# Two classical groups of gate and up instead of three, twelve by seven products; VectorE or GpSimd chosen while the list is made

## The chip, the cores and the metric

The kernel runs on one core of a Trainium2 chip. Its engines are TensorE (PE, with its weight loads shown apart as PEld), VectorE (DVE), ScalarE (ACT) and GpSimd (POOL), and SyncE (SP), whose queue issues the DMAs. Each engine works through its own instructions in the order in which they are written and waits on semaphores. The metric is the device time of one execution in microseconds (us), the median of several runs.

## What is computed

One transformer block in float32: 2048 tokens of 448 features, attention over a sliding window of 256 keys with 16 heads of 28, then a gated feed-forward network with 1792 inner features.

```
h = x + attention(layernorm(x)) @ wo      # wqkv: 448 -> 3*448, causal, window 256
n = layernorm(h)
out = h + (gelu(n @ w_gate) * (n @ w_up)) @ w_down   # 448 -> 1792 -> 448
```

## The kernel before

Every float32 operand of a matmul is held as a high part and a low part (`to_hi` on ScalarE, `to_lo` on VectorE or GpSimd: the rest that the high part leaves), and a product is the sum of three matmuls: high by high, high by low, low by high.

**The list.** The kernel first describes all its work as operations (`op(engine, cost, latency, key, function, reads, writes, ...)`) with tokens for what each reads and writes. Then `Lists.run` makes the order: it keeps a clock for each engine, takes the operation that can begin first (among those that can begin nearly at once, the one with the smallest key) and writes its instructions. The order of every engine is thus a result of the costs and keys in the table of constants at the top. Where PE would stand idle early on, `idle` puts in a 128 x 128 transpose that computes nothing (line 1720). An operation marked `port` is kept from beginning while the other of VectorE and GpSimd holds the port between them, by the list's clock.

**The stages.** Layer norm of the 16 token tiles and transposition into `xT` (`layer_norms`, `normalise`); projections to q and k (line 678) and values (line 624); 16 blocks of scores, maxima, exponentials and sums (lines 729, 802, 840), whose parts are keyed against each other; output projection (line 900), which is added to `hres` on VectorE (line 903). `MERGE` says for each of the last twelve blocks whether its attend step runs in one piece or two.

**The feed-forward network** goes through 14 groups, each a pair of 128-feature slices of gate and up for 1024 tokens (2 x 512). A group is done in one of two ways:

- Classical (the first `CL` groups): four turns, each one of gate or up for 512 tokens. A turn is seven slots of six matmuls on half the rows (`cslot`, line 1139), or full-height ones in the first three turns (`cfull`, line 1151). The weights come as sets `cw_set` and the tokens through `tokens_c`.
- By seven products (all others): one level of a Strassen-like scheme over 2 x 2 blocks, so that two units (gate and up) share 25 slots of two products each, three pairs of matmuls in a slot (`both`, line 1340). It needs sums of tokens (`tokens_x(0)` for the first 1024 tokens, `tokens_x(1)` for the others) and sums of weights (`weight_set`: five sums `sum_` at line 1210 on GpSimd, then five splits), and it adds up partial products from the banks: `copied` on ScalarE (1346), `added` on VectorE (1350), `finished`.

Both ways end in the same step: gelu(gate) * up is split into `gh`, `e` or `xT` buffers and multiplied by the down weights (`down_half`, line 1414), in halves of 12 matmuls that are put between the slots (`pause`), and `out_add` (line 1431, VectorE) adds four banks to `hres` and stores them when they are final. `seen` (line 1260) is a one-element ScalarE read that tells the change of a bank from one half of the array to the other.

The buffers of the tokens for the first round of products lie in `late`, which opens only when all attention and output projections are through (token `fp`); a weight set may come into `proj` or `ev` only when the token `wosfree` says the same of the output projection:

```
opened = ["evenring", "wvfree", "pkfree", "wosfree"]
key0 = key
for k in parts:
    key = key0 + (0 if cp else XSTEP * k)
```

## Time and profile before

| | us |
|---|---|
| median of 3 runs (696.35 to 698.05) | 696.68 |
| the profiled execution | 698.2 |
| its span, first to last instruction | 696.5 |
| PE busy | 685.1 |
| VectorE busy | 513.4 |
| ScalarE busy | 413.9 |
| GpSimd busy | 311.1 |

The profiled execution lies 1.5 us above the median, and 1.7 us of it lie outside its span. The page's busy time is a mean over stages; it is to be read with the stretches of the kernel: the start (0 to 14 us), attention (to about 300), the mix of the last attention blocks with the classical groups (300 to 376), the seven-product groups (to 674) and the tail. In a timeline's row stand the start, the length, the engine, the line and operation, what is written from what, the count, and in brackets the idle time ahead and what ended it. In the chain of waits a row of PE without a row of another engine ahead of it waited for nothing but PE itself.

### The profile page before, as it was taken

Reading aid. Unit: us, or ns where it says so; the run is one execution under the profiler, and the core shown is the slowest. Engines: PE = TensorE matmul, PEld = TensorE weight load, DVE = VectorE, ACT = ScalarE, POOL = GpSimd, SP = SyncE. Lnnn points to the kernel's source line nnn. Section 1 sums busy time; section 2 is a strip of 40 time slices with the busy share of each in tenths; the row PEclk is TensorE's granted clock in tenths of the full one; section 3 lists DMA queues with packets and bytes.
Section 4 is the critical chain, followed back from the end, with each engine's and each line's share of the span. In section 5 each row is a group of like instructions: output and inputs, shape, how many; then the busy total and the mean of one; then the engine's idle time right before and its main releaser. Section 6 shows DMA issues by size and latency. Waiting matters only on the chain. (4 is left out here: it accounts for less than half of the span.)

```text
span 696.5 us, 15373 instructions
## 1 busy us (share of the span) xinstructions
PE 685.1 (98%) x5544; PEld 578.1 (83%) x5544; DVE 513.4 (74%) x1213; ACT 413.9 (59%) x911; POOL 311.1 (45%) x422
## 2 busy tenths in 40 slices
PE   8999999999999999999999999999999999999997
PEld 7888888888888878878878888888888888888886
DVE  7967678987798788838775789776555756866764
ACT  7747576877768667776554565644534545546431
POOL 5612654644456446441452779634303445447000
PEclk9999999999999999999999999999999999999999
DMA  9997967688688697406767775415004744533102
GB/s 315 277 285 216 286 173 202 183 230 244 166 210 247 183 273 207 165 1 178 197 181 158 213 205 170 119 51 171 20 16 131 211 132 132 161 116 88 44 15 105
DMA packets 104691, 116.25 MB, mean 167 GB/s; under 512 B 44632, under 2 KB 82392, under 8 KB 104040
## 3 DMA queue, kind: packets, MB, share of 16 engines
q1 hardware_dynamic: 104472, 115.17, 58.0%
q8 instruction: 43, 0.70, 0.4%
q14 instruction: 32, 0.26, 0.1%
q10 hardware_dynamic: 144, 0.11, 0.0%
HBM read 84.97 MB, written 44.47 MB: 186 GB/s over the span
## 5 line engine op out<-in xcount | busy, mean ns | idle before, releaser
L733 DVE CUSTOM_DVE_ANT_0 mt<-bank,mt 128x384 bf16<-128x384 f32 (+2 forms) x256 | 126.4, 526 | 26.8 <-PE bank L729 24.8
L806 ACT ACTIVATE pp<-bank 128x384 f32<-128x384 f32 (+1 forms) x188 | 90.8, 527 | 18.5 <-PE bank L802 16.3
L678 PE MATMUL bank<-xT 128*128 128x512 f32 x308 | 96.1, 399 | 0.0
L1340 PE MATMUL bank<-xT,proj 64*128 64x512 f32 x735 | 94.7, 389 | 0.2 <-DVE v L1350 0.2
L1340 PEld LDWEIGHTS bank<-xT,proj 64*128 64x128 f32 x735 | 72.1, 184 | 13.4 <-DVE v L1350 0.8
L729 PE MATMUL bank<-rk,rq 84*128 84x384 f32 (+2 forms) x256 | 81.0, 337 | 0.0
L802 PE MATMUL bank<-rq,rk 104*128 104x384 f32 (+2 forms) x352 | 80.6, 302 | 0.0
L821 POOL TENSOR_SCALAR_AFFINE_SELECT pp<-pp 128x512 f32<-128x512 f32 x96 | 60.6, 651 | 40.2 <-ACT pp L806 38.6
L1414 PE MATMUL bank<-proj,gh 64*128 64x448 f32 x624 | 71.5, 362 | 1.2 <-ACT e L1260 1.2
L802 PEld LDWEIGHTS bank<-rq,rk 104*128 104x128 f32 x352 | 59.4, 190 | 9.3 <-ACT pp L806 1.5
L1431 DVE TENSOR_TENSOR hres<-bank,hres 128x448 f32<-128x448 f32 (+1 forms) x113 | 62.8, 611 | 5.6 <-PE bank L1414 5.6
L1414 PEld LDWEIGHTS bank<-proj,gh 64*128 64x128 f32 x624 | 59.2, 184 | 8.0 <-ACT e L1260 1.9
L678 PEld LDWEIGHTS bank<-xT 128*128 128x128 f32 x308 | 55.6, 189 | 6.8 <-DVE proj L399 0.5
L1210 POOL TENSOR_TENSOR xn<-proj 64x128 f32<-64x128 f32 (+2 forms) x36 | 33.3, 928 | 52.5 <-DMA proj<-gu 46.8
L1260 ACT ACTIVATE e<-bank 1x1 f32<-1x1 f32 x139 | 21.7, 156 | 55.9 <-PE bank L1414 41.3
L729 PEld LDWEIGHTS bank<-rk,rq 84*128 84x128 f32 x256 | 47.6, 189 | 7.0 <-DVE mx L733 1.4
L396 ACT ACTIVATE rq<-bank 8x512 fp32r<-8x512 f32 x64 | 37.7, 589 | 22.1 <-PE bank L760 21.0
L399 DVE TENSOR_TENSOR proj<-proj 128x448 fp32r<-128x448 f32 (+2 forms) x42 | 25.8, 630 | 32.0 <-ACT proj L396 27.0
L624 PE MATMUL bank<-proj,xT 128*128 128x448 f32 (+1 forms) x220 | 49.1, 334 | 0.0
L1340 PE MATMUL bank<-xo,proj 64*128 64x512 f32 x366 | 47.7, 389 | 0.1
L1340 PEld LDWEIGHTS bank<-xo,proj 64*128 64x128 f32 x366 | 36.0, 184 | 7.1 <-DVE v L1350 0.8
L1350 DVE TENSOR_TENSOR raw<-bank,raw 128x512 f32<-128x512 f32 x22 | 15.2, 691 | 35.1 <-PE bank L1340 35.0
(193 smaller groups left out, 1474.3 us busy)
## 6 DMA issues: line engine op xcount, KB each, us to landing
rk<-k SPq DMA_DIRECT2D x44, 336.0 KB
rq<-q SPq DMA_DIRECT2D x32, 336.0 KB
gu<-in_gu_dram SPq DMA_DIRECT2D x18, 480.0 KB
proj<-gu SPq DMA_DIRECT2D x24, 288.0 KB
q<-proj SPq DMA_DIRECT2D x12, 448.0 KB
proj<-down SPq DMA_DIRECT2D x22, 224.0 KB
proj<-gu SPq DMA_DIRECT2D x24, 192.0 KB
k<-proj SPq DMA_DIRECT2D x9, 448.0 KB
```

The lines of the kernel that those rows point to most:

```text
L396: nc.scalar.activation(dst, src, AF.Copy)
L624: op("pe", mm(224 * n), 0.29 if n == 1 else 0.38, key + a / 16, lambda a=a, h=h, wb=wb, xb=xb: nc.tensor.matmul(bank[b.k][:, 0:224 * n], x ...
L678: op("pe", mm(512) + 0.002, 0.403, key, lambda a=a, h=h, wb=wb, xb=xb: nc.tensor.matmul(bank[b.k], wqk[m][:, h, wb, :], xT[:, xb, cc * 128 ...
L729: nc.tensor.matmul(bank[b.k][:, o:384], rq[u][0:3 * DH, j, i * 128:i * 128 + 128], rk[u][0:3 * DH, j, m0 * 128:(i + 3) * 128], start=True, ...
L733: nc.vector.tensor_tensor_reduce(junk[s % 2][:, o:384], bank[b.k][:, o:384], mask[:, o:384], 1.0, -BIG, OP.add, OP.max, mx[:, i, j:j + 1])
L802: nc.tensor.matmul(bank[b.k][:, n * i:n * i + n], rk[u][0:104, j + i, m * 128:m * 128 + 128], rq[u][0:104, j + i, lo * 128:(hi + 1) * 128] ...
L806: nc.scalar.activation(pp_cols(o, n)[:, j:j + G], bank[b.k][:, 0:G * n].rearrange("p (g t) -> p g t", g=G), AF.Exp, scale=SCALE)
L821: nc.gpsimd.affine_select(a, a, pattern=[[0, 4], [-cm, 128]], compare_op=op_, fill=0.0, base=0, channel_multiplier=cm)
L1210: arith("pool", w, key + 1, lambda e: e.tensor_tensor(xn_m[HALF[side], o:o + w], a(), b(), op=what), rd, [tok])
L1340: nc.tensor.matmul(bank[b.k], w, xarea(u.cp, xl, xs, side)[:, xk], start=p in (1, 2, 5) and not k and not t, stop=t == 2, tile_position=(6 ...
L1414: nc.tensor.matmul(bank[banks[q].k][:, 0:D], h[oh][0]()[HALF[x], q * 128:q * 128 + 128], d[wh][0]()[HALF[x]], start=not ph and not y and n ...
L1431: op("dve", 0.07 + w * 0.463 / D, 0.163 + w * 0.463 / D, key, lambda: nc.vector.tensor_tensor(hres[:, t, c0:c0 + w], bank[b.k][:, c0:c0 + ...
```

## The change

1. `CL` goes from 3 to 2: one group less is done classically and one more by seven products. The first product slot stands earlier in PE's order. The rings of buffers are arranged anew (`wbuf`, `cgbuf`, `SPARE`), and part of the token areas of the first round now lies in `xT` (`XPLACE`), where some of its loads may be made before attention ends (`X0LOAD`, `X0HOLD`).
2. An operation can have `alts`: engines with a cost each. The list then chooses the one on which it would end first; GpSimd counts only if no VectorE operation that holds the port began later than GpSimd could begin. `FLEX = 'xwc'` says for which: token sums and splits (x), weight sums and splits (w), copies from banks (c, ScalarE or VectorE).
3. Layer norm of the first tile (`QUICK = 1`): VectorE subtracts and scales in one instruction from the mean itself, so that one GpSimd step is left out.
4. The high and low halves of `xT` have tokens of their own (`XTB`), so that values and projections wait for the half that each matmul reads.
5. The list's cost for a DMA is changed, and nearly all keys in the table of constants are others.

```diff
-MERGE = (1, 1, 1, 0, 1, 1, 1, 1, 0, 1, 1, 1)
+MERGE = (1, 1, 1, 0, 1, 1, 1, 1, 1, 0, 0, 1)
...
-CL = 3
-CWL = 100
+FLEX = 'xwc'
+CL = 2
+CWL = -50
...
+QUICK = 1
+XFIRST = 4
...
+        if alts:
+            o.fn = lambda: alts[o.eng][2]()
...
+                if o.alts:
+                    ways = [x for x in o.alts if x != "pool" or began <= max(free[x], o.ready) + 0.02]
+                    if e not in ways or min(start_of(x, o)[0] + o.alts[x][1] for x in ways) < t + o.alts[e][1]:
+                        continue
...
-                bus = max(bus, t + 1.2) + o.size * 0.0034 + (1.25 if len(dmas) == 2 else 0)
+                bus = max(bus, t + 1.2) + o.size * (0.0028 if t < 15 else 0.0034) + (1.0 if len(dmas) == 2 else 0)
...
+                if e == "dve":
+                    began = t
...
+    def XTB(t, xb):
+
+        return span("xT", t, 1) if xb == 3 else span("xT", t + (xb > 3) / 2, 0.5)
...
+        if kind == "ln1" and t < QUICK:
+            op("dve", 0.45, 0.53, key, lambda: nc.vector.tensor_scalar(
+                xn[i2], hres[:, t, :], bnmv[:, i4, 0:1], bnve[:, 1, i4:i4 + 1], op0=OP.subtract, op1=OP.mult),
+               [HR(t), ("bnve", i4), ("bnmv", i4)], [XN(i2)])
...
-    cgbuf0, cubuf0, cgbuf = [*RAW, *EV], [VM[6], XNB], [*VM[3:7], EV[1]]
+    cgbuf0, cubuf0, cgbuf = [*RAW, *EV], [VM[6], XNB], [VM[4], *VM[0:4]]
...
+    wbuf = wbuf if CL > 2 else [wbuf[2], *wbuf[:2]]
...
-    def arith(eng, n, key, fn, r, w, port=True):
-        cost = 0.1 + n * 0.00225 if eng == "pool" else 0.07 + n * 0.00104
-        op(eng, cost, cost + (0.05 if eng == "pool" else 0.1), key, lambda: fn(nc.gpsimd if eng == "pool" else nc.vector),
-           r, w, port=port)
+    def arith(eng, n, key, fn, r, w, port=True, free_choice=False):
+        ways = {"pool": (0.1 + n * 0.00225, 0.15 + n * 0.00225, lambda: fn(nc.gpsimd), port),
+                "dve": (0.07 + n * 0.00104, 0.17 + n * 0.00104, lambda: fn(nc.vector), port)}
+        cost, lat, go, _ = ways[eng]
+        op(eng, cost, lat, key, go, r, w, port=port, alts=ways if free_choice else None)
...
-            arith("pool", w, key + 1, lambda e: e.tensor_tensor(xn_m[HALF[side], o:o + w], a(), b(), op=what), rd, [tok])
+            arith("pool", w, key + 1, lambda e: e.tensor_tensor(xn_m[HALF[side], o:o + w], a(), b(), op=what), rd, [tok], free_choice="w" in FLEX)
```

What it does to the order is seen at three places. The names are those of the code; `bank_...` is a PSUM bank, `pp` holds raw weights, `w` is the ring of buffers in `ev`.

**PE, the start.** Before, from the last fillers ahead of the first value product to the first projections (line 454 transposes a normalised tile, 624 multiplies values, 678 projects, 1720 is the filler):

```order
L1720 MATMUL bank_177<-ident 128x128
L624 MATMUL bank_176<-proj,xT 128x224 x6
L454 MATMUL bank_178<-ident,xn 128x128 x4
L454 MATMUL bank_179<-ident,xn 128x128 x4
L624 MATMUL bank_176<-proj,xT 128x224 x5
L624 MATMUL bank_177<-proj,xT 128x224 x11
L1720 MATMUL bank_176<-ident 128x128
L624 MATMUL bank_175<-proj,xT 128x224 x8
L678 MATMUL bank_178<-xT 128x512 x11
```

The same place now (the lines are 484, 658, 712 and 1762):

```order
L1762 MATMUL bank_175<-ident 128x128
L484 MATMUL bank_177<-ident,xn 128x128 x4
L658 MATMUL bank_175<-proj,xT 128x224 x9
L658 MATMUL bank_176<-proj,xT 128x224 x3
L484 MATMUL bank_174<-ident,xn 128x128 x4
L484 MATMUL bank_177<-ident,xn 128x128 x4
L658 MATMUL bank_176<-proj,xT 128x224 x5
L658 MATMUL bank_175<-proj,xT 128x224 x2
L658 MATMUL bank_176<-proj,xT 128x224 x3
L712 MATMUL bank_173<-xT 128x512 x3
```

The value products stand right behind the second tile's transposes, and the projections begin after 22 of them instead of 30. In all PE's order has 17 fillers where it had 29.

**GpSimd, the weight sets.** Before, all five sums of a set and some splits stand on GpSimd (line 1210 sums, 399 splits, 1057 is a token sum):

```order
L1210 TENSOR_TENSOR xn<-w_3359,xn 128x384
L1210 TENSOR_TENSOR xn<-w_3359 64x128
L1210 TENSOR_TENSOR xn<-w_3359,xn 64x384
L1210 TENSOR_TENSOR xn<-w_3359 64x384
L399 TENSOR_TENSOR w_3359<-xn,w_3359 128x384
L1210 TENSOR_TENSOR xn<-proj 64x128
L1210 TENSOR_TENSOR xn<-proj 128x384
```

Now its order has, from the last attention selects on (line 1248 sums, 446 to 454 are a layer norm's):

```order
L855 AFFINE_SELECT raw<-raw 128x512
L1248 TENSOR_TENSOR xn<-proj 128x384
L1248 TENSOR_TENSOR xn<-w_3351 128x384
L1248 TENSOR_TENSOR xn<-w_3351 64x128
L1248 TENSOR_TENSOR xn<-w_3351,xn 128x384
L446 TENSOR_SCALAR bnve<-bnmv 128x2
```

Of 90 weight sums before, all were GpSimd's; of 100 now, 13 are. GpSimd has 331 instructions that were 427, VectorE 1343 that were 1215.

**VectorE, from the output projection to the products.** Before, behind the last add of the output projection (903), layer norms of later tiles (428, 490) follow and then the first token sums:

```order
L903 TENSOR_TENSOR hres<-bank_178,hres 128x448
L399 TENSOR_TENSOR gh<-raw,gh 128x512 x2
L399 TENSOR_TENSOR xT<-e_3360,xT 128x512
L399 TENSOR_TENSOR e_3363<-e_3361,e_3362 128x512
L490 STREAM_TRANSPOSE v<-v 128x448
L428 BN_STATS bnst_76<-hres 128x6
L430 BN_AGGR bnmv<-bnst_76 128x2
L428 BN_STATS bnst_77<-hres 128x6
```

Now, at the end of the stretch that must be through before the down matmuls behind the first three product slots (425 splits, 1092 and 1095 are token sums, 1217 is the classical gate times up, 1473 frees a down bank into `hres`):

```order
L425 TENSOR_TENSOR proj<-xn,proj 128x384
L1092 TENSOR_TENSOR raw<-raw,xT 64x512
L1217 TENSOR_TENSOR v<-bank_170,v 128x512
L1217 TENSOR_TENSOR v<-bank_171,v 128x512
L1095 TENSOR_TENSOR e_3352<-xo,raw 64x512
L425 TENSOR_TENSOR xT<-xT,xo 128x512
L425 TENSOR_TENSOR xT<-raw,xo 128x512
L425 TENSOR_TENSOR xo<-e_3352,xo 64x512
L425 TENSOR_TENSOR gh<-v,gh 128x512
L1473 TENSOR_TENSOR hres<-bank_174,hres 128x448
L1473 TENSOR_TENSOR hres<-bank_175,hres 128x448
```

The first of these splits feeds PE's first product slots, and the adds into `hres` at the end stand behind all three rounds of token sums of the first 1024 tokens. From the first add of the output projection to the second of these adds there are 57 VectorE instructions.

More of the change, by code (lines that the diff above doesn't have):

```diff
@@ L415, in layer_norms @@
         i, n = ts[0] % 4, len(ts)
+        quick = kind == "ln1" and ts[0] < QUICK
         def ve():
@@ L679, in project_tile @@
                 bank[b.k], wqk[m][:, h, wb, :], xT[:, xb, cc * 128:cc * 128 + 512], start=(a == 0),
-                stop=(a == NP - 1)), [span("xT", cc, 4), WQK(m, h)], (), b, tag="proj")
+                stop=(a == NP - 1)), [*(XTB(cc + i, xb) for i in range(4)), WQK(m, h)], (), b, tag="proj")
         proj_ops[c, m] = L.ops[-NP:]
@@ L1009, in load @@
         def load(l, slot, side, c, row, k0=0, n=1):
-            dma(key, 131 * n, lambda: nc.sync.dma_start(f(xarea(cp, l, slot, side)[:, k0:k0 + n]), rows(c, row + 64 * k0, n)),
+            soon = not cp and type(XPLACE[cp][l, slot]) is tuple
+            dma(X0LOAD + 10 * k0 if soon else key, 131 * n, lambda: nc.sync.dma_start(
+                f(xarea(cp, l, slot, side)[:, k0:k0 + n]), rows(c, row + 64 * k0, n)),
                 come(c) + xgate(cp, l, slot), [t for k in range(k0, k0 + n) for t in xtok(cp, l, slot, k, side)], cost=0.61 + 0.03 * n,
-                after=chain[-1:])
+                after=[got[X0HOLD]] if soon else chain[-1:])
         def fill(k, i, c, row):
```

170 lines of the change are left out of this document (94 added, 76 removed).

## The prediction

> **What bounds the kernel now.** I read the page's first block, then the busy time by stage, then the chain of waits, then the timelines of the places where the chain leaves TensorE.
>
> ```profile
> span 696.5 us, 15373 instructions
> PE 685.1 (98%) x5544; PEld 578.1 (83%) x5544; DVE 513.4 (74%) x1213; ACT 413.9 (59%) x911; POOL 311.1 (45%) x422
> ```
> ```profile
> 0.00:14.00 14.00, 10.56 (x75) 9.80 (x76) 9.59 (x21) 10.13 (x17) 9.61 (x29) 1.00 0.87 298
> 50.00:300.00 250.00, 249.95 (x1792) 205.39 (x1791) 204.17 (x674) 180.32 (x358) 123.23 (x205) 1.00 0.75 211
> 300.00:376.30 76.30, 74.36 (x636) 60.33 (x636) 50.88 (x91) 45.78 (x109) 26.91 (x33) 1.00 0.60 151
> 376.30:674.00 297.70, 297.01 (x2698) 256.51 (x2696) 207.01 (x325) 152.39 (x377) 138.94 (x131) 1.00 0.41 120
> 674.00:696.50 22.50, 17.25 (x147) 14.85 (x145) 12.53 (x23) 3.50 (x13) 0.00 (x0) 0.96 0.23 82
> ```
>
> The columns after the length are the busy us of PE, PEld, DVE, ACT and POOL. TensorE is the bound: attention (50 to 300) has no gap. So a change can win by taking matmuls away, by starting sooner, or by removing the short waits between 300 and 674; and it can lose by making new waits.
>
> **Term 1, the matmuls removed: -2.1 us.** The chain of waits, in order of time, gives the price of each kind of work:
>
> ```profile
> 355.87 4.81 PE bank L1139 x42
> 399.42 2.74 PE bank L1340 x24
> 402.16 1.21 PE bank L1414 x12
> 403.38 2.06 PE bank L1340 x18
> 454.31 2.74 PE bank L1340 x24
> 481.22 2.74 PE bank L1340 x24
> 671.25 2.75 PE bank L1340 x24
> ```
>
> A classical group has four turns of 42 matmuls: 4 x 4.81 = 19.24 us. A seven-product group has 25 slots of 6 matmuls, which the chain shows as seven runs of 18 and one of 24: 7 x 2.06 + 2.74 = 17.16. The products with down are the same number. One group changes kind: 17.16 - 19.24 = -2.1 us, all on the path, since PE is the bound on both sides. This term is sure.
>
> **Term 2, the start: -1.0 us.**
>
> ```profile
> 2.14 3.67 PE L1720 MATMUL bank<-ident 128*128 128x128 f32 x18 [2.14 <-POOL ident L550]
> 8.31 1.15 PE L1720 MATMUL bank<-ident 128*128 128x128 f32 x9
> 9.21 1.10 PE L624 MATMUL bank<-proj,xT 128*128 128x224 f32 x6
> 14.07 0.40 PE L678 MATMUL bank<-xT 128*128 128x512 f32 x1
> 5.65 0.76 ACT L449 ACTIVATE xn<-hres,bnve 128x448 f32<-128x448 f32 x1 [1.76 <-POOL bnve L422]
> ```
>
> L1720 are fillers that compute nothing. The nine at 8.31 stand where PE waits for both halves of xT; the new dependencies let the first value products go on the high half alone, and none of these fillers is left in the new order (29 become 17). Their place, 9.21 - 8.31 = 0.9 us, is won, and some tenths more because tile 0 skips one GpSimd step and goes to VectorE instead of the 0.76 us at 5.65. The wqk loads are the far bound: three hres loads are now queued on SP ahead of the third wqk load, and if PE waits for it, the gain is nothing. Ends: 0 and -1.6; I take -1.0, near the row of fillers.
>
> **Term 3, the way from attention into the products: +0.6 us.** Before, PE loses time there three times, each time in the second half of a down pair:
>
> ```profile
> 318.56 0.37 PE L900 MATMUL bank<-proj 128*128 128x448 f32 x1
> 322.27 0.37 PE L900 MATMUL bank<-proj 128*128 128x448 f32 x1
> 336.99 1.37 PE L1414 MATMUL bank<-proj,gh 64*128 64x448 f32 x12
> 338.85 1.50 PE L1414 MATMUL bank<-proj,gh 64*128 64x448 f32 x12 [0.48 <-ACT e L1260]
> 352.23 1.37 PE L1414 MATMUL bank<-proj,xT 64*128 64x448 f32 x12
> 354.37 1.50 PE L1414 MATMUL bank<-proj,xT 64*128 64x448 f32 x12 [0.77 <-ACT e L1260]
> 367.75 1.37 PE L1414 MATMUL bank<-proj,gh 64*128 64x448 f32 x12
> 369.81 1.48 PE L1414 MATMUL bank<-proj,gh 64*128 64x448 f32 x12 [0.69 <-ACT e L1260]
> 376.28 2.23 PE L1340 MATMUL bank<-xo,w 64*128 64x512 f32 x18
> ```
>
> Twelve such matmuls take 1.21, so the starts are late by 338.85 - 336.99 - 1.21 = 0.65, then 0.93 and 0.85, and each restart costs 0.1 more (1.50 against 1.37): 2.75 us in all. The change removes the group with two of them, but moves the first seven-product slot from 376 to about 346 (27 classical slots and 48 down matmuls, 18.6 + 4.8 us, behind the output projection that ends at 322.6), and all token sums, splits and the first weight set must be made by then. That work stands on VectorE:
>
> ```profile
> 318.96 0.63 DVE L903 TENSOR_TENSOR hres<-bank,hres 128x448 f32<-128x448 f32 x1 [1.47 <-PE bank L900]
> 319.50 0.68 DVE L1179 TENSOR_TENSOR raw<-v,raw 128x512 f32<-128x512 f32 x1
> 320.10 0.69 DVE L1179 TENSOR_TENSOR raw<-xn,raw 128x512 f32<-128x512 f32 x1
> 347.09 1.69 DVE L1431 TENSOR_TENSOR hres<-bank,hres 128x448 f32<-128x448 f32 x3
> ```
>
> From start to start an instruction of 512 columns takes 0.60 and one of 448 some 0.55 (1.69 / 3). In the new order 57 VectorE instructions stand from the first add of the output projection (here at 318.96) to the second add that frees a down bank: 35 of 512 columns, 12 of 448, 6 of 384 (about 0.5) and 4 small (about 0.2): 21.0 + 6.6 + 3.0 + 0.8 = 31.4 us. PE needs less for what stands between the same two points: three more blocks of the output projection (322.27 - 318.56 = 3.7), 27 classical slots at 4.81 / 7 (18.6), 48 down matmuls (4.8) and three product slots (2.06), 29.2 us. The add starts 0.3 after the block, so PE waits 31.4 + 0.3 - 29.2 = 2.5 us, and about 0.8 more for the next two banks, whose adds follow at 0.55 each. Thus 3.3 us of wait replaces 2.75. Below, nothing of it shows and all old waits go (-2.7); above, the DMAs are late too (+4, rival B).
>
> **Term 4, the seven-product groups: -1.4 us.** Between the rows at 399.42 and 671.25 lie ten groups, 271.83 us; the one from 454.31 to 481.22 took 26.91. So ten groups lose 2.7 us. A part of them lies where VectorE meets GpSimd:
>
> ```profile
> 433.46 2.74 DVE L399 TENSOR_TENSOR xT<-v,xT 128x512 fp32r<-128x512 f32 x1
> 433.11 1.29 POOL L399 TENSOR_TENSOR xT<-xT 128x512 fp32r<-128x512 f32 x1
> 434.37 1.28 POOL L399 TENSOR_TENSOR xT<-v,xT 128x512 fp32r<-128x512 f32 x1
> L399 DVE TENSOR_TENSOR gh<-v,gh 128x512 fp32r<-128x512 f32 x26 | 23.5, 903 | 5.4 <-ACT gh L396 5.3
> ```
>
> A VectorE instruction with two SBUF inputs, 0.68 at 319.50, lasted 2.74 beside two GpSimd instructions; the 26 splits of gh have a mean of 903 ns. The change moves 87 of the 100 weight sums, and more splits, to VectorE, which lengthens its queue by about half a microsecond each, yet takes the partner of these collisions away. [...] I take half the old loss as gone: -1.4. Ends: -2.7 (all gone) and +5 (rival A).
>
> **Term 5, attention and the tail: +0.3 us.** One more attend group is cut in two (ten ones in MERGE become nine); each change of tile shape costs the 0.1 seen above at a restart, two or three of them. The engines' orders are re-keyed throughout, but PE has no gap there to win; the adds, loads and selects are the same ones, hidden under a PE that is busy 249.95 of 250. If this cover failed somewhere, up to 1 us. The tail after 674 keeps its shape.
>
> **Sum:** -2.1 - 1.0 + 0.6 - 1.4 + 0.3 = -3.6. The profiled execution took 698.2 (span 696.5 and 1.7 around it), so 694.6 by it; the median of the runs is 696.68, 1.5 lower, which gives 693.1.
>
> **Rivals.** A, slower: VectorE becomes the bound of the early groups.
>
> ```profile
> 646.90:674.00 27.10, 27.10 (x248) 23.48 (x246) 15.79 (x27) 11.59 (x28) 0.00 (x0) 1.00 0.14 37
> ```
>
> The last group, with GpSimd idle and no preparation, needs 15.8 of VectorE's 27.1. Two weight sets of sums add about 4.2, and their splits and two thirds of the second round of token sums (14 instructions of 0.6) some 8: 28 against 26.9. That is 1.1 too much in the fullest group. If the first six groups lose that much each, in place of the gain of term 4, the time is 693.1 + 1.4 + 6.6 = 701.1; it decides from 0.7 us a group (693.1 + 1.4 + 4.3 = 698.8). For it: the sums are now on the engine that also empties the banks PE waits for. Against: later groups have slack, and a busy VectorE is no wait by itself. [...] Chance 0.16.
>
> B, no change: the first weight set or the token loads come late.
>
> ```profile
> 348.30 1.23 SPq L1196 DMA_DIRECT2D w<-gu  x2
> 354.29 1.01 POOL L1210 TENSOR_TENSOR xn<-w 128x384 f32<-128x384 f32 x1 [8.54 <-DMA w<-gu]
> 362.84 1.17 POOL L399 TENSOR_TENSOR w<-xn,w 128x384 fp32r<-128x384 f32 x1 [0.79 <-ACT w L396]
> ```
>
> Six microseconds from issue to use, and ten more until GpSimd's last split of this set ends at 364.0: 16. Now these loads may start only when the output projection is through (322.6), with some twenty others on SP, and 23 us are left until 346. VectorE does the sums in half the time, which speaks against B; the queue on SP speaks for it. Three more microseconds there and no gain at the start give 693.1 + 3 + 1 = 697.1. Chance 0.20.
>
> C, the forecast: the terms as summed, 690.0 to 694.6. Chance 0.64.
>
> **Range and chances.** Less than 0.3% (2.1 us) can't be told from no change here. Faster 0.64 (C), same 0.20 (B), slower 0.16 (A). C alone is 690.0 to 694.6: the terms' good ends together would give 688, which I count 1 in 20. For 8 in 10 the range goes through B: 690.0 to 698.8.
>
> **What would show it.** Term 1: 1820 product matmuls at a clean group of 26.9, and twelve x24 rows. Term 2: the first project matmul near 12.5 to 13 in place of 14.07, no block of fillers after the second transposes. Term 3: one wait of 2 to 3 us on VectorE's adds of hres behind the first three product slots, and VectorE without a gap for 30 us before it. Term 4: no VectorE split over 2 us; POOL below 45% by far; gh splits near 0.7 us. It would be wrong if the six early groups took over 28 us each, or if PE waited on a DMA of gu before its first slot.

## The result, and the profile after

The changed kernel takes 707.41 us (median of 6 runs, 702.72 to 708.62) where the kernel before takes 697.57 (6 runs, 696.35 to 698.05, the three of the table above among them): a ratio of 1.0133, interval 1.0111 to 1.0154. It is 1.3% slower; the forecast of 693.1 us and its whole range, 690.0 to 698.8, lie below it. The profiled execution of the changed kernel took 704.3 us against 698.2.

The first block of its page:

```profile
span 702.4 us, 15242 instructions
PE 687.0 (98%) x5514; PEld 597.2 (85%) x5514; DVE 557.1 (79%) x1341; ACT 413.6 (59%) x907; POOL 202.5 (29%) x326
```

PE is the bound as before. GpSimd gave up 109 us of work, VectorE took 44. To see where 5.9 us of span went, I cut both traces at the same landmarks of PE: the first projection, the last output projection, the first down matmul, the first seven-product slot, the point where eleven product groups are left. Here are the stretches by stage, of the changed kernel and then, from the output projection on, of the one before (columns as in the prediction):

```profile
12.68:322.85 310.17, 308.31 (x2163) 253.59 (x2162) 245.47 (x778) 216.71 (x428) 145.05 (x245) 1.00 0.77 213
322.85:338.93 16.08, 16.08 (x142) 13.04 (x141) 14.81 (x26) 10.40 (x25) 1.01 (x1) 1.00 0.93 211
338.93:351.34 12.41, 9.65 (x75) 7.76 (x72) 11.59 (x22) 7.15 (x17) 1.25 (x1) 0.86 0.20 49
380.37:702.39 322.02, 315.65 (x2844) 290.96 (x2841) 250.94 (x450) 155.12 (x386) 34.50 (x38) 1.00 0.42 120
```
```profile
322.27:336.99 14.72, 14.72 (x129) 11.91 (x128) 12.80 (x26) 9.07 (x21) 6.53 (x10) 1.00 0.83 233
376.28:696.46 320.18, 314.28 (x2843) 271.38 (x2839) 219.56 (x348) 155.89 (x390) 138.94 (x131) 1.00 0.40 117
```

| stretch, us | before | after | difference |
|---|---|---|---|
| start and attention, to the last output projection | 322.27 | 322.85 | +0.58 |
| from there until eleven product groups are left | 54.01 | 57.52 | +3.51 |
| the last eleven groups and the tail | 320.18 | 322.02 | +1.84 |
| span | 696.46 | 702.39 | +5.93 |

The matmuls saved (2.06 us) are in these numbers: twelve classical ones (1.37) are missing ahead of the last output projection, the other 0.69 in the second stretch. So the waits grew by 1.95 us at the start and in attention, by 4.2 in the second stretch and by 1.84 at the end. Each has its own rows. One execution of run 8 below took 2907 us, in the slow state, and is left out of its median.

**The way into the products.** PE's timeline between the first down matmul and the first product slot, then two rows from just behind it:

```profile
338.93 1.37 PE L1456 MATMUL bank<-proj,gh 64*128 64x448 f32 x12
340.83 0.88 PE L1456 MATMUL bank<-proj,gh 64*128 64x448 f32 x6 [0.53 <-ACT e L1299]
343.94 1.49 PE L1456 MATMUL bank<-proj,gh 64*128 64x448 f32 x6 [2.23 <-ACT e L1299]
345.23 3.84 PE L1177 MATMUL bank<-xT,w 64*128 64x512 f32 x24
348.90 2.60 PE L1456 MATMUL bank<-proj,gh 64*128 64x448 f32 x24
351.34 0.39 PE L1380 MATMUL bank<-xo,proj 64*128 64x512 f32 x2
...
354.01 2.47 PE L1456 MATMUL bank<-proj,xT 64*128 64x448 f32 x12 [0.45 <-DVE hres L1473]
356.11 0.60 PE L1380 MATMUL bank<-xo,proj 64*128 64x512 f32 x2
```

24 classical and 48 down matmuls stand in these 12.41 us, and by the prediction's durations they need 4.81 x 24 / 42 + 4 x 1.21 = 7.6: 4.8 us are lost. Two waits of 0.53 and 2.23 are on ScalarE's one-element read of a bank (`seen`). Most of the rest is slow PE: the 24 classical matmuls took 3.84 us instead of 2.90 (their time in run 2), the six down matmuls ahead of them 1.49 instead of 0.88. The same stretch by windows of two microseconds, whose eighth column is the granted clock:

```profile
342.00:344.00 2.00, 0.06 (x2) 0.06 (x2) 2.00 (x5) 1.43 (x4) 0.00 (x0) 0.95 0.03 7
344.00:346.00 2.00, 2.00 (x10) 1.75 (x12) 2.00 (x4) 1.48 (x3) 0.00 (x0) 0.50 0.14 38
346.00:348.00 2.00, 2.00 (x16) 1.57 (x14) 1.91 (x5) 0.62 (x2) 0.00 (x0) 0.70 0.11 41
```

The clock went to half (0.50) behind two waits of 2.76 us in all, with 0.88 of work between. The half clock lasted from 343.80 to 347.21, 3.41 us; in the 3.41 us ahead of it PE was busy for 0.88.

Why the reads came late is seen on three queues: SP's issues, VectorE, ScalarE.

```profile
324.24 1.09 SPq L1234 DMA_DIRECT2D w<-gu  x2
325.43 0.54 SPq L1048 DMA_DIRECT2D xo<-xn  x1
...
335.17 0.69 DVE L425 TENSOR_TENSOR xo<-e,xo 128x512 fp32r<-128x512 f32 x1 [1.24 <-ACT xo L422]
...
333.99 0.63 ACT L422 ACTIVATE xo<-xo 64x512 fp32r<-64x512 f32 x1 [1.40 <-DMA xo<-xn]
343.20 0.63 ACT L422 ACTIVATE xo<-e 128x512 fp32r<-128x512 f32 x1 [0.17 <-DVE e L1095]
343.74 0.14 ACT L1299 ACTIVATE e<-bank 1x1 f32<-1x1 f32 x1
```

Two loads of the second weight set (590 KB) were issued at 324.24, ahead of the token loads. ScalarE waited for a token load (1.40), VectorE for ScalarE (1.24). From there to 348.49 VectorE has no gap in which it could catch up. Eight microseconds later ScalarE stands at a token split that waits for VectorE, with the read that PE needs queued behind it until 343.74.

**The product groups.** From the first slot on the groups took 29.03, 27.45, 27.27, 30.55 and then 26.87 four times (before: 26.93, 27.6, 27.29, 26.9, 27.53, 26.9, ...). The first, fourth and fifth by stretch:

```profile
351.34:380.37 29.03, 28.40 (x247) 24.09 (x245) 25.26 (x51) 15.61 (x40) 12.49 (x18) 1.00 0.69 178
435.09:465.64 30.55, 29.11 (x250) 23.80 (x248) 28.28 (x47) 17.00 (x39) 8.30 (x7) 1.00 0.45 134
465.64:492.51 26.87, 26.87 (x250) 23.05 (x247) 20.40 (x37) 11.57 (x29) 2.18 (x3) 1.00 0.34 98
```

In the fourth, VectorE is busy for 28.28 us where PE needs 26.87. PE loses 2.4 us of its 3.7 too many at the first down pair of that group, behind a VectorE split that takes 1.51 us (the shortest split into `w` takes 0.42):

```profile
435.42 1.51 DVE L425 TENSOR_TENSOR w<-w 128x256 fp32r<-128x256 f32 x1
...
438.12 2.46 PE L1456 MATMUL bank<-proj,gh 64*128 64x448 f32 x12 [0.58 <-DVE hres L1473]
```

The pair waits for the adds that free its banks (the next slot begins at 440.90, 1.57 late, and 0.86 are lost ahead of the pair). So it does in the first group at 354.01. There 0.61 us are lost ahead of it and 0.89 in it (356.11 - 354.01 - 1.21): 1.5 of that group's 2.2.

**The start.** Two rows of before, then DVE's casts (629), GpSimd's clears (619, 623), SP's load of a slice of wqk and what waited for it, on ScalarE and then PE:

```profile
13.11 1.13 PE L624 MATMUL bank<-proj,xT 128*128 128x224 f32 x8
...
14.25 1.03 DVE L595 CAST rk<-e 8x768 fp32r<-8x768 f32 x2
```

```profile
12.88 3.12 POOL L619 MEMSET rk<- 32x1536 f32 x2
...
13.92 2.50 DVE L629 CAST rk<-e 8x768 fp32r<-8x768 f32 x2
...
17.20 0.33 SPq L667 DMA_DIRECT2D raw<-in_wqk_dram  x1
...
17.97 2.26 POOL L623 MEMSET rq<- 32x1024 f32 x2
...
18.40 2.25 DVE L629 CAST rk<-e 8x768 fp32r<-8x768 f32 x2
...
22.20 0.63 ACT L422 ACTIVATE xT<-raw 128x512 fp32r<-128x512 f32 x1 [2.53 <-DMA raw<-in_wqk_dram]
...
22.88 0.50 PE L712 MATMUL bank<-xT 128*128 128x512 f32 x1 [1.46 <-ACT xT L422]
```

The first projection does come 1.4 us earlier (12.68 for 14.07). But the eight value products that took PE from 13.11 to 14.07 before now stand behind it, so only 0.43 us of this is won, and at 22.88 PE gives 1.46 back. The same two casts, which took 1.03 us before, take 2.50 and 2.25 beside clears; the split that frees the buffer of that load stands behind them on VectorE.

**Runs and profile.** Over 12 runs of this kernel, (1 - mean granted clock) x 700 us averages 3.0 us; over 11 runs of the kernel before it is 0.8. A straight line of time on that number has a slope of 0.85 (correlation 0.77). So some 2 us of the 9.8 us between the medians go with half-clock time, more than the profiled execution, at a mean clock of 0.997, shows; runs at a clock of 1.000 still took 702.72 and 705.91. A part of that spread is attention: in eight profiles (this one and runs 1 to 7), in which PE's order is the same up to there, the last output projection came at 322.17 to 324.27.

### The profile page after: what moved, and what is told of

Same layout as the page of the kernel before. It is cut to its first block, busy times and chain, and to the rows that moved or that the text cites. A ratio compares the mean times of both kernels' runs of the same rounds, so it can differ in the third digit from the quotient of the medians.

```text
span 702.4 us, 15242 instructions
## 1 busy us (share of the span) xinstructions
PE 687.0 (98%) x5514; PEld 597.2 (85%) x5514; DVE 557.1 (79%) x1341; ACT 413.6 (59%) x907; POOL 202.5 (29%) x326
## 5 line engine op out<-in xcount | busy, mean ns | idle before, releaser
L1380 PE MATMUL bank<-xT,proj 64*128 64x512 f32 x627 | 123.6, 388 | 0.0
L1380 PE MATMUL bank<-xo,proj 64*128 64x512 f32 x552 | 113.0, 389 | 0.3 <-DVE v L1387 0.3
L1380 PEld LDWEIGHTS bank<-xT,proj 64*128 64x128 f32 x627 | 83.7, 184 | 4.2
L1456 PE MATMUL bank<-proj,gh 64*128 64x448 f32 x672 | 83.6, 366 | 3.5 <-ACT e L1299 2.8
L1380 PEld LDWEIGHTS bank<-xo,proj 64*128 64x128 f32 x552 | 73.1, 184 | 7.0 <-DVE v L1387 0.7
L1456 PEld LDWEIGHTS bank<-proj,gh 64*128 64x128 f32 x672 | 70.1, 185 | 10.0 <-ACT e L1299 3.5
L1380 PE MATMUL bank<-xT,w 64*128 64x512 f32 x330 | 64.9, 388 | 0.0
L1380 PE MATMUL bank<-xo,w 64*128 64x512 f32 x255 | 55.1, 388 | 0.3 <-DVE raw L1392 0.3
L1380 PEld LDWEIGHTS bank<-xT,w 64*128 64x128 f32 x330 | 44.6, 184 | 2.3
```

Source lines behind the costliest of these rows:

```text
L1380: nc.tensor.matmul(bank[b.k], w, xarea(u.cp, xl, xs, side)[:, xk], start=p in (1, 2, 5) and not k and not t, stop=t == 2, tile_position=(6 ...
L1456: nc.tensor.matmul(bank[banks[q].k][:, 0:D], h[oh][0]()[HALF[x], q * 128:q * 128 + 128], d[wh][0]()[HALF[x]], start=not ph and not y and n ...
```

## The experiments

My theory was that four separate waits cost what the change saves: the late loads, the half clock behind the wait, VectorE's demand in the fourth group, and the casts beside clears. The rivals were that VectorE's work is too much throughout (A), that its meetings with GpSimd are what lengthens it, and that the loss is one wait that moves on when it is removed. In the edits `t` is the list's clock and `o.fn()` the place where `Lists.run` writes an instruction, so work is moved in the order (added in run 2, left out in run 4) and nothing else. All were timed in five rounds; ratios are against the kernel before, in runs on the same chip.

**1. The changed kernel again**, without an edit.

> The changed kernel once more, for its spread and a second profile. Its runs lay between 702.7 and 708.6 us where those before lay within 1.7 us, and the mean granted clock of TensorE went from 1.000 (702.7) to 0.992 (708.4). Theory: the runs differ mainly by how long TensorE runs at half clock after its wait at 340 to 346 us, so this profile has the same waits (about 2.8 us at 340 to 344, a fourth seven-product group of some 30.5 us, 1.5 us at 22.9) and a time that goes with its clock. Rival: the waits themselves differ from run to run by 2 us or more, and the clock by little.

706.65 us, ratio 1.0128 (1.0100 to 1.0155). The waits were the same ones (0.38 and 2.34, a fourth group of 30.56), and the 24 classical matmuls took 4.50 us. The order's waits repeat. The half clock lasted 3.41 us again, but lay 1.3 us later (345.06 to 348.47) and so fell on more of these matmuls.

**2. Fillers in the wait**

```diff
-            o.fn()
+            [idle(t, t + 9, dict(bank_free)) for _ in range(18 if 336.7 < t < 336.8 else 4 if 335.2 < t < 335.25 else 0)] if e == "pe" else 0; o.fn()
...
-        if t > WARM or t + cost > until or not ks:
+        if t > WARM and until < t + 8 or t + cost > until or not ks:
```

> Adds 22 transposes that compute nothing on TensorE where it waits inside the down pair ahead of the product slots (4 ahead of the first late half, 18 ahead of the second), 22 x 0.109 = 2.4 us of work in 2.8 us of wait. Theory that the low clock comes from the idle time: the granted clock stays at 1.00 from 342 to 348, the 24 classical matmuls behind take 2.75 us in place of 3.84, and the kernel wins 1.6 us on the profile and 1 to 4 on the median. Rival, the clock falls by the load or by chance: the clock is as low as before and the time the same or up to 0.5 us longer.

705.60 us, 1.0117 (1.0084 to 1.0150). 22 transposes that compute nothing stand in the waits. In the profile the clock held, by the same windows:

```profile
342.00:344.00 2.00, 1.40 (x11) 0.92 (x11) 1.94 (x5) 1.10 (x4) 0.00 (x0) 1.00 0.01 2
344.00:346.00 2.00, 2.00 (x20) 1.93 (x18) 2.00 (x5) 1.40 (x4) 0.00 (x0) 1.00 0.02 6
346.00:348.00 2.00, 2.00 (x20) 1.65 (x20) 2.00 (x4) 1.97 (x4) 0.00 (x0) 1.00 0.17 47
```

The 24 classical matmuls took 2.90. But the stretch from first down to first slot was 12.10 us for 12.41: the fillers themselves pushed the second half of the down pair 0.7 us later. That the clock falls because PE idles is supported (0.50 from 344 to 346 without the fillers, 1.00 with them); that holding it is worth anything by itself is not.

**3. Two loads moved behind the first set's**

```diff
-        began = 0.0
+        began, held = 0.0, []
...
-            o.fn()
+            held.append(o.fn) if e == "sp" and o.key == 1415 and 318 < t < 319 else o.fn(); [held.pop(0)() for _ in held[:] if e == "sp" and o.key == 1480 and t > 325.6]
```

> Two DMAs of the second weight set (590 KB in all), which stand on SyncE's queue ahead of the token loads of the first products, are issued behind the loads of the first weight set instead; nothing else moves. Theory that late loads set the wait ahead of the products: the token areas land 2 to 2.5 us sooner, VectorE loses its gap of 1.24 us at 335, and the waits of TensorE at 340 to 344 (2.8 us) shrink by 1 to 2.5 us. Rival, the length of VectorE's queue sets it: the loads come sooner, the waits stay within 0.4 us. Against both: the second set, issued late, could stall the slots near 365.

702.32 us (701.78 to 704.04), 1.0066 (1.0049 to 1.0083): half of the loss, from the place of two DMAs.

```profile
335.22 0.68 DVE L425 TENSOR_TENSOR xo<-e,xo 128x512 fp32r<-128x512 f32 x1
...
332.47 1.24 SPq L1234 DMA_DIRECT2D w<-gu  x2
...
343.36 0.88 PE L1456 MATMUL bank<-proj,gh 64*128 64x448 f32 x6 [0.83 <-ACT e L1299]
348.51 1.48 PE L1456 MATMUL bank<-proj,gh 64*128 64x448 f32 x12 [0.32 <-ACT e L1299]
349.83 0.39 PE L1380 MATMUL bank<-xo,proj 64*128 64x512 f32 x2
```

VectorE has no gap at 335 any more, nor anywhere from 321.9 to 349; the waits are 0.83 and 0.32; the clock stays at 1.00; first down to first slot takes 9.55 us for 12.41. From the last output projection on the profile is 2.9 us shorter; its span gains only 1.5, since in this execution attention ended at 324.21 for 322.85, ahead of the edit. The median gains 4.3 against run 1 on the same chip, and the runs spread over 2.3 us instead of 6.3.

**4. Layer-norm work taken off VectorE.** Two transposes, two statistics and one aggregate are left out between 316 and 326.

```diff
-            o.fn()
+            o.fn() if not (e == "dve" and o.key in (1850, 1851, 1950, 1951) and 316 < t < 326) else None
```

> Leaves out five VectorE instructions and one aggregate of the layer norm of two later tiles (two stream transposes, two statistics, one aggregate), which stand among the adds of the output projection and the first token splits; their tiles then hold stale numbers. Some 4 x 0.55 + 0.1 = 2.3 us less on VectorE ahead of the first products. Theory that VectorE's queue sets the wait: TensorE's waits at 340 to 344 shrink by 1.5 to 2.3 us. Rival, the loads set it: VectorE waits longer for the token areas and the waits shrink by less than 0.5 us.

704.41 us, 1.0103 (1.0073 to 1.0133). First down to first slot fell to 10.06 us, with waits of 1.33 and 0.33. Less work on VectorE ahead of the token sums shortens the same wait that earlier loads shorten: VectorE is a link of that chain.

**5. The second round of token sums spread otherwise**

```diff
-XTIME = (8, 7, 8)
+XTIME = (10, 6, 8)
```

> The three parts of the second round of token sums, which the changed kernel makes during two neighbouring units (the fourth seven-product group, 30.55 us in the profile), are spread to the units 10, 6 and 8. Theory that VectorE has too much work in that group: it falls to 27 to 28 us, others rise by 0.3 at most, and the kernel wins 2 to 3.5 us. Rival, single collisions with GpSimd set it: the loss moves to another group and the sum over the early groups stays within 1 us.

**6. The ten GpSimd operations of the fourth and fifth group on VectorE**

```diff
-            o.fn()
+            o.eng = "dve" if o.alts and e == "pool" and 420 < t < 456 else e; o.fn(); o.eng = e
```

> The ten operations that GpSimd has in the fourth and fifth seven-product group (token sums, splits) are written for VectorE at the same place; nothing else moves. Theory that the amount of work on VectorE sets the long group: ten more instructions of some 0.55 us, less 3.4 us of collisions (four VectorE instructions of 1.5 to 1.8 in place of 0.68), so 2 us more on VectorE, and the group is as long as before or up to 1.5 us longer. Rival, the collisions alone make it long: they are gone, and the group falls by 2 to 3.5 us.

5 gave 706.43 us, 1.0142 (1.0104 to 1.0181), 6 gave 707.23, 1.0136 (1.0114 to 1.0159). The fourth group in 5, then in 6:

```profile
436.38:465.50 29.12, 28.72 (x250) 24.18 (x247) 28.79 (x50) 17.40 (x41) 6.91 (x7) 1.00 0.47 133
```
```profile
437.62:468.55 30.93, 28.86 (x251) 23.11 (x248) 28.18 (x52) 17.10 (x39) 0.00 (x0) 1.00 0.45 133
```

In 6 GpSimd stands still and the group is no shorter; the fifth grows from 26.87 to 27.80. So it isn't the meetings with GpSimd by themselves that make the group long (the changed kernel has three around here: VectorE instructions of 1.79 us at 431.94, 1.51 at 435.42 and 1.78 at 447.16): with their work on VectorE instead, VectorE is as busy (28.18 us) and the group as long. Nor does that total fix the length: in 5 VectorE is busy for 28.79 us and the group is 1.4 us shorter, though not the 27 to 28 that were expected, and the third 0.24 longer. Which work stands ahead of the adds and splits that PE waits for counts too. The median of 5 did not follow: in that profile the half clock of the transition lasted from 343 to 350, which took the gain. Only with the transition mended (run 10) could it be seen.

**7. The first set's four sums on GpSimd again**

```diff
-            o.fn()
+            o.eng = "pool" if o.alts and e == "dve" and o.key == 1481 and t < 336 else e; o.fn(); o.eng = e
```

> Four sums of the first weight set go back from VectorE to GpSimd, which is idle there (338 to 342 us); nothing else moves. They took VectorE 0.29 + 0.56 + 0.56 + 0.55 us. Theory that the sums moved to VectorE make the wait ahead of the products: VectorE is 1.9 us sooner through, and TensorE's waits at 340 to 344 shrink by 1 to 2 us. Rival, that the two engines hinder each other when both read SBUF: four GpSimd sums of about 1 us double the VectorE instructions beside them, the first set is ready later, and the kernel loses 0 to 2 us.

706.97 us, 1.0133 (1.0111 to 1.0156). The two waits became one of 3.45, and first down to first slot took 13.22 us. Taking four sums off VectorE does not make it sooner: on GpSimd they took some 4.2 us (its busy time from 300 to 351 is 13.79 for 9.54) where VectorE had taken 1.96, and VectorE then waited 0.91 us for them, until 340.57.

**8. GpSimd's four clears behind three layer-norm steps**

```diff
-            o.fn()
+            held.append(o.fn) if e == "pool" and o.key == 0 and 15.8 < t < 21 else o.fn(); [held.pop(0)() for _ in held[:] if e == "pool" and t > 25]
```

> Four GpSimd clears of 32 rows (two of 1536, two of 1024 columns), which lie beside VectorE's casts at 13.9 and 18.4 us, are put behind three GpSimd steps of layer norm; nothing else moves. Theory that the start loses its gain by this meeting: the casts take 1.05 us a pair in place of 2.50 and 2.25, the buffer of the third and fourth wqk slice comes free 1.4 us sooner, the wait of TensorE at 22.9 us (1.46) falls below 0.3, and the kernel wins 1 to 2 us. Rival, the queue of loads ahead of these slices sets the wait: the casts are short and the wait stays above 1 us.

703.41 us (702.73 to 711.62, 5 runs), 1.0101 (1.0060 to 1.0143).

```profile
13.86 1.03 DVE L629 CAST rk<-e 8x768 fp32r<-8x768 f32 x2
15.68 0.33 SPq L667 DMA_DIRECT2D raw<-in_wqk_dram  x1
20.80 3.36 PE L712 MATMUL bank<-xT 128*128 128x512 f32 x14
```

A pair of casts takes 1.03 us, the load goes out 1.52 earlier, and the wait at 22.88 is gone; the last output projection comes at 321.80 for 322.85. That last step alone would not show a gain, since the same place varied from 322.17 to 324.27 without the edit and from 321.08 to 323.75 in the four profiles with it (this run and 10, 11 and 14). The wait does: from the first projection to 26 us PE is idle for 1.0 to 1.7 us in the eight profiles without the edit and for 0.00 in these four. By what means clears that only write lengthen the casts (2.50 and 2.25 beside them, 1.03 and 1.03 here) no run shows; the `port` of the code is a rule of the list, not a measurement. In this profile waits of 0.62 and 2.47 stood at the transition, and yet the clock stayed at 1.00.

**9. The start alone, on the kernel before:** `QUICK` and `XTB`, nothing else.

```diff
-PKX = (2, 3)
+PKX = (2, 3); QUICK = 1
...
+    def XTB(t, xb):
+
+        return span("xT", t, 1) if xb == 3 else span("xT", t + (xb > 3) / 2, 0.5)
...
```

> The kernel before with only the changed start: tile 0 normalised on VectorE, and the two halves of xT waited for apart; all keys, groups and engines as before. Theory that the start itself is worth about 1 us: the first project matmul comes at 12.2 to 13.3 us in place of 14.07, and the kernel takes 0.5 to 1.5 us less than before. Rival: the time won is given back at the next wqk slice or in attention, as in the changed kernel (its first project matmul stood at 12.68, its output projection ended 0.6 us later than before), and the time is within 0.5 us of before or above it.

700.78 us, 1.0049 (1.0030 to 1.0069): slower than before. The first projection came at 12.18, 1.9 earlier (0.96 of it by the eight value products that here too moved behind it), but the last output projection at 325.73, 3.5 later; after that everything took as long as before (53.49 and 320.13). The list made another order of attention from the earlier start, and that order waits, at 27.38 and 205.42 among others:

```profile
27.38 0.63 PE L460 MATMUL bank<-ident,xn 128*128 128x128 f32 x4 [0.80 <-ACT pp L400]
205.42 0.67 PE L812 MATMUL bank<-rq,rk 104*128 104x128 f32 x4 [0.96 <-ACT rq L400]
```

**10. Edits 3, 5 and 8 together**

> Three edits together on the changed kernel: the second weight set's two loads behind those of the first, the four clears behind three steps of layer norm, the second round of token sums spread to units 10, 6 and 8. Alone they moved the profile by -2.8 us (output projection to eleven groups left), -1.1 (start to output projection) and -1.2 (the last eleven groups). If these are three separate waits, the sum is -5.1: a profile of about 699.4 and a median of 698 to 700, with TensorE's clock at 1.00 between 338 and 351. Rival, the waits hide one another: less than 3.5 us together.

700.06 us (10 runs, 698.90 to 703.47), 1.0036 (1.0020 to 1.0052). On the profile: last output projection at 321.08, first down to first slot 9.81 us, fourth group 29.13, span 697.0. The three gains add up (-5.4 us of span for the -5.1 expected), so the three waits are separate. This is the best version run, and it is still 0.36% above the kernel before.

**11. Run 10, and two statistics and an aggregate behind the transition**

> As the combination, and two statistics and an aggregate of a later layer norm (1.2 us of VectorE) are moved from between the first token splits to behind the adds of hres. With the load moved, VectorE has no gap from 322 to 349, so if its queue is what is left of the wait, TensorE's waits ahead of the first product slot fall by 0.8 to 1.2 us against the combination. Rival, ScalarE's order sets the rest: less than 0.3 us.

702.30 us, 1.0069 (1.0043 to 1.0095). First down to first slot went to 9.66; the waits on the reads of the banks are 0.64 and 0.63 where run 10 had 0.81 and 0.63, so VectorE's queue is no longer what sets them, as the rival had it. The first group went from 29.06 to 30.30, with a new wait of 1.1 on VectorE's adds (1392): what is moved out of one place there makes a wait in another.

**12. Weight sums and splits on the table's engines** (GpSimd's, as before)

```diff
-FLEX = 'xwc'
+FLEX = 'xc'
```

> The changed kernel with the weight sums and splits on the engines that the tables give (sums on GpSimd), token sums and copies still chosen in the list; the list is made anew. Theory that VectorE has too much to do because of the weight sums: its busy time in the first group falls from 24 to 16 us, that group and the fourth take 27.0 to 28 us each in place of 29.03 and 30.55, and the kernel is 2 to 5 us faster than the changed one in spite of a later first slot. Rival, that two engines on SBUF cost more than they bring: VectorE's instructions get longer, the groups stay above 28, and the time is the same or longer.

707.78 us, 1.0142 (1.0121 to 1.0163): not the gain of 2 to 5 us that was expected.

```profile
359.03 1.69 PE L1380 MATMUL bank<-xo,proj 64*128 64x512 f32 x4 [5.27 <-DVE proj L425]
```

The first weight set is 5.27 us late, the first group takes 35.70, and the clock falls there (0.89 in the mean over this group). But the next three groups, the fourth among them, take 27.34, 27.49 and 27.48, the fourth with VectorE busy for 26.82 us. So the free choice is needed for the first set, and it adds to VectorE's work in the fourth group (28.28 us for 26.82).

**13. Three classical groups with the rest of the change.** The buffers stay as they are arranged for two, so the numbers that come out are not those of the block; only the time is read.

```diff
-CL = 2
-CWL = -50
+CL = 3
+CWL = 100
```

> The changed kernel with three classical groups (and their key CWL as before); engines still chosen in the list, the start as changed. It puts 2.06 us of matmuls back. Theory that the way into the products is too short with two: the first slot comes at 375 or later, the wait in the down pair ahead of it is under 1 us, TensorE's clock stays at 1.00 there, the first seven-product group takes under 28 us in place of 29.03, and the time is 1 to 4 us less than the changed kernel's in spite of the added work. Rival, the choice of engines and the start make the loss, whatever the number of groups: the time is that of the changed kernel plus 1 to 3 us.

703.04 us (701.51 to 709.68), 1.0089 (1.0058 to 1.0120). With 2.06 us more of matmuls it is some 3 us (by the ratios) to 4 us (by the medians) faster than the changed kernel, where the rival had 1 to 3 us more; the intervals still overlap a little. It is 0.9% slower than before, so two groups in place of three are not the whole loss. The first product slot comes at 379.47, the waits at the down pairs are 1.48 and 0.94, the first group takes 27.21; now the second takes 29.91, with VectorE busy for 28.00.

**14. Edits 3 and 8, and a free choice for the first two sets only**

```diff
...
-                free_choice="w" in FLEX)
+                free_choice=n < 2)
```

> The changed kernel with the second set's loads and the four clears moved as in the combination, and the weight sums and splits chosen in the list for the first two sets alone, on the tables' engines (sums on GpSimd) from the third on. Theory that VectorE's load makes the fourth group long, and GpSimd's slowness only the first set late: the fourth group takes 27.5 (as with all sums on GpSimd) in place of 30.55, the first stays at 29 to 29.8, and the profile is 697 to 699, at least 1 us below the combination's median of 700.06. Rival, the two engines hinder each other as much as VectorE's load did: groups two to four take 28 or more each and the time is that of the combination or longer.

701.69 us, 1.0053 (1.0033 to 1.0074), not the 1 us below run 10 that was expected. The first four groups took 28.97, 28.51, 27.86 and 27.73, 113.1 us; in run 10 they took 113.2. The excess is spread, not removed, although VectorE is busy there for 96.99 us in place of 100.83 and GpSimd for 59.33 in place of 28.56. So less work on VectorE alone does not shorten these groups, and the rival, that the two engines hinder each other as much, is not out.

## Why the prediction was wrong

It foresaw -3.6 us on the profiled execution; +5.9 came in the span, and the median lies 3.1 above the profiled execution besides. Step by step:

**Term 1 (-2.1) was right.** 1800 product matmuls for 1650 (the prediction's own count of 1820 for this was a slip), and undisturbed groups of 26.87: -2.06.

**Term 2 (-1.0) and 5 (+0.3): together +1.95 measured.** PE's first projection came where the prediction said (12.68), with 17 fillers, but that sign was met by luck: 0.96 us of the 1.39 are the eight value products that moved behind it, which the prediction did not count, and 0.43 were won in place of 1.0. It had named the right far bound, the wqk load, but set its loss at "nothing gained" and put the cause on SP's queue. The cause lay on VectorE, in casts beside clears (run 8), and the loss was 1.46. The order puts the clears and the casts next to each other, and no row of before showed a cast longer than 1.05. Term 5 was sized by PE having no gap in attention. Run 9 shows why that argument doesn't hold: the list makes attention's order anew from any other start, and the new one can have gaps that the old one had not. In run 8, without the wait at 22.88, the way from the first projection (12.16) to the last output projection (321.80) takes 309.6 us; before it took 308.2 with 1.37 more of classical matmuls and 0.96 less of value products. So 1.9 us of small losses remain there, and they take back what the start won. In that profile PE waits 0.9 us at a transposition for ScalarE, 0.5 for a load of k and 0.2 for ScalarE again; before it has no wait in attention that the view lists.

**Term 3 (+0.6) is the step that failed most: +4.2.** The prediction had the right place, the second halves of the down pairs and the adds of `hres`, and the right engine, VectorE. Its 3.3 us of waits assumed a VectorE without a gap for 30 us. Where that assumption is made true (run 3), 9.55 - 7.6 = 1.95 us are lost ahead of the first slot and 29.06 - 26.87 = 2.2 in the first group: 4.1, near the 3.3. In the changed kernel 4.8 + 2.2 = 7.0 were lost. The difference is rival B's mechanism, late token loads behind 590 KB of a weight set that nobody needs yet, worth 2.9 us on the trace (12.41 - 9.55). B had 0.20 and a price of 3: the size was right, but it was held against the forecast as a rival when it had to be added to it. The wait that was forecast, on VectorE's adds of `hres` behind the first product slots, is there as well, but with 1.5 us, in the first group; the other 2.6 of the 4.1 lie elsewhere, so that the closeness to 3.3 is in part luck. Inside the 2.9 is the half clock, of which the prediction had no term. It cost about 1.5 us in this profile (3.84 for 2.9 and 1.49 for 0.88, the six down matmuls ahead), 1.6 in run 1 on the 24 alone (4.50). Run 2 kept the clock up and won no more than 0.3 us on this stretch, so this part is not shown to be worth its 1.5 us by itself.

**Term 4 (-1.4): +1.84.** Its better half came: the splits of gh fell from 903 to 686 ns, no split takes over 1.51 us where one took 2.74, and the groups from the fifth to the eighth lose nothing (26.87). Without the fourth group's 3.68 us too much, the last eleven groups and the tail would be 1.84 us shorter than before, more than the 1.4 forecast. That group is what the term left out. Rival A's arithmetic came true as well, in one group instead of six: 28 us of VectorE's work against 26.9 was its figure for the fullest group, 28.28 the trace's. But this group, with 1.4 us too much, is 3.7 too long. Where PE waits in it is seen: for the adds that free its banks (438.12) and for adds and splits further on. Why the waits come to more than the excess is not shown; the order on VectorE has a part in it (run 5). Here is how the chain of waits enters its last unbroken stretch on PE, at 461.57 in the fourth group:

```profile
459.22 1.69 DVE proj L425 x3
460.92 0.61 DVE raw L1392
461.53 0.04 issue
461.57 3.01 PE bank L1380 x24
```

Three weight splits stand ahead of the add that PE waits for. The few meetings with GpSimd that are left are not by themselves what makes the group long (run 6).

**The sum.** Of the 9.5 us between -3.6 and +5.9, terms 2 and 5 make 2.65, term 3 makes 3.6 and term 4 makes 3.25. The other 4.8 us up to 707.4 lie in the step from profile to median: the prediction took 1.5 off, since the profiled run of before took longest of its runs, while the changed kernel's was 3.1 below its median. With all terms but the first missed in the same direction, the range of 690.0 to 698.8 was too narrow above: B and A were priced as alternatives, and both happened, beside the half clock.

What stays open: the first group's 2.2 us, which no run with two classical groups removed; why the fourth group loses more than VectorE's excess; why the waits in attention differ between executions of one order, by up to 2.1 us at the last output projection; and whether another order would keep what the start won.

## What to carry to other kernels

When work moves to an engine that frees what the bound engine waits for, compare its demand with the bound engine's time in each window between two meeting points, not over the kernel: 28.3 us against 26.9 in one group cost 3.7 here, though 28.8 in another order cost 2.3 (run 5), so the window tells where to look and not the price. On an in-order queue ask what stands ahead of the urgent item: two loads nobody needed yet cost 2.9 us here, and moving them gave 4.3 in the median; a part of the difference goes with the clock, whose mean loss, (1 - mean granted clock) x 700 us, fell from 3.5 us in run 1 to 0.7 in run 3. And where a list or planner makes the order, an earlier start is a new order: its gain holds only if the stages behind it are looked at again, and rivals with different places add up.

## What the runs showed of the hardware that I had not expected

- At the transition the granted clock fell to 0.50 for 3.41 us or twice that, behind a longest wait of 1.99 (run 12) to 3.45 us (run 7), and did not fall behind one of 2.47 in run 8. The fall at the kernel's end stands 358.40 us behind the one at the transition in the changed kernel's profile, and 354.98, 358.40 and 358.41 in those of runs 1, 5 and 7: 104 or 105 times 3.413. Counted in such steps back from the fall, the step just ahead of it had PE busy for 0.15 to 1.71 us in the six profiles with such a fall (0.88 in the changed kernel's; the first fall in run 12); in run 8, counted back from the fall at the kernel's end, the wait is divided between two steps with 1.92 and 1.82. So what counts seems to be where the wait lies in these steps. The bound is not shown: over the first 14 us the mean granted clock was 0.88 in runs 12 and 13, with PE busy for 10.16 and 10.44 us, and 1.00 in the changed kernel's profile, with PE busy for 10.27. Short transposes in the wait held the clock at 1.00 (run 2).
- A pair of VectorE casts of 8 x 768 from float32 took 2.50 us beside GpSimd clears and 1.03 with the clears moved (run 8).
- The place of two DMA issues took the spread of the runs from 6.3 us (run 1) to 2.3 (run 3). But runs 4, 11 and 14 spread over 7.8, 8.0 and 6.3 us without a wait over 1.33 us at the transition in their profiles, so a long wait there is not the whole cause of the spread.
